# Windowed attention followed by a gated channel mix: some transposes moved to the DMA crossbar, casts moved between engines, deeper pools, a split last product, and another order

## The chip, the cores and the metric

The kernel runs on one core of one Trainium2 chip. The metric is the time of one execution on the device in microseconds (us), median of several runs; lower is better. The profile is one more execution under the hardware profiler, and its span runs from the first to the last instruction, so it is about 1.7 us shorter than the time of the same run. Engines are PE (TensorE, with PEld for its weight loads), DVE (VectorE), ACT (ScalarE), POOL (GpSimd) and SP (the engine whose queue issues most DMAs). A run counts as slow when it is over 1.5% above the fastest of its kernel, else as fast; ratios use fast runs alone.

## The reference

```python
# q, k, v: (4, 8, 768, 64) f32; window 128, 4 sink positions; weights w_k 512x1024, w_v 1024x512, w_r 512x512
scores = where(keep, q @ k.T / 8, -1e9)       # keep: first 4 positions, or 0 <= row - col < 128
a = softmax(scores);  x = heads side by side of (a @ v)          # (4, 768, 512)
x_prev = x shifted down by one row in each batch
xk = mu_k*x + (1-mu_k)*x_prev;  xr = mu_r*x + (1-mu_r)*x_prev
out = sigmoid(xr @ w_r) * (relu(xk @ w_k)**2 @ w_v)
```

## The kernel before

The work is cut into 12 units of 256 rows (4 batches of 3). A unit goes through: load q, k, v; cast to bf16; transpose q and k; scores, exponential, mask, values; normalise to x; transpose x; shift and mix into xk and xr; then keys (`kp`), gate (`rp`) and product (`vp`) with the weights. Every operation is registered in a plan with its engine, the buffers it takes and a number. `ORDER` lists for each engine the numbers in the order in which it issues them, and that order was found by a search beforehand. Each engine's program is written in this order, so an operation that waits holds up everything that is listed behind it.

```python
CAST = {"k": "ACT", "q": "DVE"}      # who casts k and q of units 1 to 11
KD = range(4, 12)                    # units whose k is transposed by the DMA crossbar
QD = ()                              # ... and whose q: none
ORDER = {"PE": (88, 85, 101, ...), "DVE": (...), "ACT": (...), "POOL": (...), "SP": (...)}
# ... cut
pool("sc", TOGETHER, [128, 2, 512], FP32, psum)        # TOGETHER = 2
pool("bank", 8 - 2 * TOGETHER, [128, 512], FP32, psum)
pool("kb", 2, ...); pool("qb", 2, ...); pool("kt", 3, ...); pool("qt", 2, ...); pool("e", 4, ...)
pool("es", 2, ...); pool("rec", 3, ...); pool("x", 2, ...); pool("xk", 2, ...); pool("xr", 2, ...)
pool("rl", 3, ...)
# ... cut: prepare(u), for each half of q and of k
copy(out=buf[rk][:, half], in_=buf[raw][:, hs])        # the cast, on DVE or ACT
if by_dma(name, u):                                    # the crossbar: SP issues, no engine computes
    nc.sync.dma_start_transpose(out=buf[key][:, :, half, :], in_=buf[rk][:, half])
    continue
nc.tensor.transpose(out=ps[:, i, j, :], in_=..., identity=ident)   # four of them on PE, then
nc.scalar.copy(out=buf[key][...], in_=buf[psk][...])               # the evacuation on ACT
# ... cut: ffn(u), for each half g of the rows
for f in range(4 * part, 4 * part + 4):                # product: 8 matmuls of 512 columns
    nc.tensor.matmul(out=buf[psk], rhs=wv_h[:, f, :], lhsT=buf["kk", u][:, f, 128*g:128*g+128], ...)
nc.vector.scalar_tensor_tensor(out=buf[bk], in0=buf[tk], scalar=1.0, in1=buf[psk],
                               op0=ALU.add, op1=ALU.mult)
nc.sync.dma_start(out=out[b, s0:s0 + 128, :], in_=buf[bk])
# ... cut: where the plan sees PE idle in the first 45 us and a PSUM bank free, it puts a filler
P.fill = lambda bank: nc.tensor.matmul(out=bank, lhsT=warm[:, 0:128], rhs=warm, start=True, stop=True)
```

The softmax here doesn't subtract the row's maximum and nothing guards it: scores larger than these inputs give would overflow.

## Time and profile before

| | before |
|---|---|
| time, median | 178.24 us of 3 runs; 177.93 us of 4 beside the changed kernel |
| span of the profile | 177.0 us (that run took 178.66 us) |
| busy: PE, DVE, ACT | 164.5, 154.3, 127.4 us |
| mean granted clock of PE | 0.977 |
| packets on the DMA engines, share of 16 engines' span | 75% on the main queue |

How to read it: PE's busy share is high, but it adds up matmuls that overlap: a key product lasts 276 ns on the mean, and in full stretches the next one starts 109 ns later.

### The profile page before, as it was taken

How to read it: one execution, taken by the hardware profiler on the slowest of the kernel's cores; microseconds unless marked ns; L12 is line 12 of the kernel's file. 1: busy time of each engine (PE TensorE's matmuls, PEld its weight loads, DVE VectorE, ACT ScalarE, POOL GpSimd, SP SyncE). 2: the span in 40 equal slices, each digit the busy share in tenths (PEclk: the TensorE clock that was granted, in tenths of full speed). 3: DMA queues.
4: the chain of work that ended last, by engine and by line, in shares of the span. 5: the costliest groups of instructions: out<-in, count | busy, mean ns of one | idle time of the engine just before them, and what ended most of it. 6: DMA issues, size and time to landing. Idle time of an engine off the chain costs nothing.

```text
span 177.0 us, 4245 instructions
## 1 busy us (share of the span) xinstructions
PE 164.5 (93%) x1619; PEld 109.8 (62%) x1640; DVE 154.3 (87%) x393; ACT 127.4 (72%) x205; POOL 25.1 (14%) x47
## 2 busy tenths in 40 slices
PE   7996579899998999999999999999999999999991
PEld 2444357685656758757657659557668577664840
DVE  6377997999999989999999998999899999778522
ACT  2168895989496995999876887888998764844240
POOL 6004100009131010114110031401120000000000
PEclk9999957999999999999999999999999999999998
DMA  5999999979957988979994799799862010040403
GB/s 150 261 226 250 346 383 386 332 180 258 232 129 191 283 117 205 235 147 265 211 264 126 201 274 249 139 240 137 225 156 70 4 59 0 4 178 0 178 4 119
DMA packets 74148, 32.79 MB, mean 185 GB/s; under 512 B 52112, under 2 KB 68496, under 8 KB 74128
## 3 DMA queue, kind: packets, MB, share of 16 engines
q1 hardware_dynamic: 73072, 32.51, 75.0%
q8 instruction: 13, 0.21, 0.5%
q10 hardware_dynamic: 1056, 0.00, 0.3%
q14 instruction: 7, 0.06, 0.1%
HBM read 24.12 MB, written 6.29 MB: 172 GB/s over the span
## 4 chain that ended last, share of the span: by engine, by line
PE 71%; DVE 17%; DMA 3%; SPq 3%; issue 2%; ACT 1%; ACTq 0%; DVEq 0%
PE bank L778 21%; PE bank L816 21%; PE bank L801 10%; PE bank L695 6%; PE sc L636 5%; DMA qs<-in_q_dram 3%; DVE xk L757 3%; DVE e L672 3%; PE bank L551 3%; PE bank L734 2%; DVE xr L757 2%; PE bank L683 2%; SPq L378 2%; DVE kk L791 2%; PE bank L612 2%
## 5 line engine op out<-in xcount | busy, mean ns | idle before, releaser
L778 PE MATMUL bank<-xk,wk_sb 128*128 128x256 bf16 x384 | 51.5, 276 | 1.9 <-DVE wk_sb L504 1.3
L658 ACT ACTIVATE e<-sc 128x1024 bf16<-128x1024 f32 (+1 forms) x48 | 45.4, 966 | 3.8 <-PE sc L636 3.7
L816 PE MATMUL bank<-wv_h,kk 128*128 128x512 bf16 x181 | 46.6, 379 | 0.5
L778 PEld LDWEIGHTS <-wk_sb 128*128 128x128 bf16 x384 | 35.8, 99 | 10.4 <-issue 1.7
L787 ACT ACTIVATE rl<-bank 128x512 bf16<-128x512 f32 x48 | 27.9, 603 | 15.8 <-PE bank L778 14.5
L576 POOL CAST vb<-vs 128x512 bf16<-128x512 f32 x22 | 17.9, 822 | 103.5 <-DMA vs<-in_v_dram 90.2
L672 DVE TENSOR_TENSOR e<-e,mask 128x1024 bf16<-128x1024 bf16 (+1 forms) x48 | 31.1, 652 | 0.5 <-ACT e L658 0.5
L816 PEld LDWEIGHTS <-kk 128*128 128x128 bf16 x192 | 17.4, 98 | 15.1
L801 PE MATMUL bank<-wr_sb,xr 128*128 128x512 bf16 x87 | 23.9, 379 | 1.0 <-ACT xt L742 0.4
L791 DVE TENSOR_TENSOR kk<-rl 128x512 bf16<-128x512 bf16 x48 | 20.8, 448 | 3.5 <-ACT rl L787 3.0
L757 DVE SCALAR_TENSOR_TENSOR xr<-td,mu,xt 128x256 bf16<-128x256 bf16 x48 | 23.5, 499 | 0.0
L757 DVE SCALAR_TENSOR_TENSOR xk<-td,mu,xt 128x256 bf16<-128x256 bf16 x48 | 22.4, 486 | 0.1
L695 PE MATMUL bank<-vb,e 128*128 128x65 bf16 x352 | 20.3, 197 | 0.8 <-ACT kt L561 0.6
L711 DVE TENSOR_TENSOR x<-bank,rec 128x256 bf16<-128x256 f32 x48 | 19.8, 418 | 0.6
L807 ACT ACTIVATE th<-bank 128x512 f32<-128x512 f32 x24 | 14.4, 612 | 8.2 <-PE bank L801 8.2
L695 PEld LDWEIGHTS <-e 128*128 128x128 bf16 x352 | 17.6, 100 | 3.3 <-DVE e L672 1.1
L825 DVE SCALAR_TENSOR_TENSOR ob<-th,bank 128x512 f32<-128x512 f32 x24 | 16.3, 680 | 3.8 <-PE bank L816 3.7
L742 ACT COPY xt<-bank 128x512 bf16<-128x512 bf16 x24 | 14.1, 590 | 5.5 <-PE bank L734 5.5
L561 ACT COPY qt<-bank 128x512 bf16<-128x512 bf16 x22 | 16.4, 748 | 1.6 <-PE bank L551 1.3
L801 PEld LDWEIGHTS <-xr 128*128 128x128 bf16 x96 | 9.0, 98 | 8.7 <-DVE xr L757 0.6
L636 PE MATMUL sc<-qt,kt 64*128 64x128 bf16 (+1 forms) x256 | 14.3, 243 | 0.0
L683 PE MATMUL bank<-vsink,es 128*128 128x130 bf16 x64 | 13.3, 229 | 0.0
(49 smaller groups left out, 153.0 us busy)
## 6 DMA issues: line engine op xcount, KB each, us to landing
vs<-in_v_dram SPq DMA_DIRECT2D x24, 256.0 KB, 5.3
out_dram<-ob SPq DMA_DIRECT2D x24, 256.0 KB, 2.5
qs<-in_q_dram SPq DMA_DIRECT2D x11, 512.0 KB, 6.0
ks<-in_k_dram SPq DMA_DIRECT2D x18, 256.0 KB, 4.7
wk<-in_moe_w_k_dram SPq DMA_DIRECT2D x2, 1024.0 KB, 10.4
wv<-in_moe_w_v_dram SPq DMA_DIRECT2D x2, 1024.0 KB, 12.9
ks<-in_k_dram SPq DMA_DIRECT2D x3, 512.0 KB, 9.1
wr<-in_moe_w_r_dram SPq DMA_DIRECT2D x1, 1024.0 KB, 10.6
```

What stands on the lines that cost most here:

```text
L576: lambda g=g, copy=copy: copy(out=buf["vb", u][:, g, :, 0:D], in_=buf["v", u][:, g, :, :]), rank,
L636: nc.tensor.matmul(out=sc[:, a, o0:o1], lhsT=lhs[rows], rhs=rhs[rows], start=True, stop=True)
L658: nc.scalar.activation(out=buf[ek][:, :, lo:], in_=buf[sck][:, :, lo:], func=AF.Exp, scale=scale)
L672: nc.vector.tensor_tensor(out=at, in0=at, in1=m, op=ALU.mult)
L695: nc.tensor.matmul(out=o[:, g, a, :], lhsT=e[:, a, e0:e0 + 128], rhs=rhs, start=(T == 0 and i == 0), stop=(i == len(blocks) - 1), skip_gro ...
L711: P.op("DVE", dve(256), lambda ok=ok, rk=rk, c=c: nc.vector.tensor_tensor(out=buf["x", u][:, :, 128 * c:128 * c + 128].rearrange("p g (a d ...
L757: nc.vector.scalar_tensor_tensor(out=buf[key][:, c0 + i, :], in0=buf[tk][:, i, :], scalar=mu[w][:, c0 + i:c0 + i + 1], in1=xt[:, c0 + i, t ...
L778: nc.tensor.matmul(out=ps[:, i, :], lhsT=wk_sb[:, c, 128 * f:128 * f + 128], rhs=xk[:, c, :], start=(c == 0), stop=(c == NC - 1), skip_gro ...
L787: P.op("ACT", act(512), lambda psk=psk, rk=rk: nc.scalar.activation(out=buf[rk], in_=buf[psk].rearrange("p (i t) -> p i t", i=2), func=AF. ...
L791: P.op("DVE", dve(512, 0.52), lambda f2=f2, rk=rk: nc.vector.tensor_tensor(out=buf["kk", u][:, 2 * f2:2 * f2 + 2, :], in0=buf[rk], in1=buf ...
L801: nc.tensor.matmul(out=buf[psk], lhsT=buf["xr", u][:, c, 128 * g:128 * g + 128], rhs=wr_sb[:, c, :], start=(c == 0), stop=(c == NC - 1))
L816: nc.tensor.matmul(out=buf[psk], rhs=wv_h[:, f, :], lhsT=buf["kk", u][:, f, 128 * g:128 * g + 128], start=(f == 0), stop=(f == NF - 1))
```

## The change

Its intent: take work off PE where PE is the bound (q of units 8 to 11 through the DMA crossbar), take casts off DVE and give them to ACT, give the order more buffers, shorten the tail, and find the order again for all this.

```diff
-CAST = {"k": "ACT", "q": "DVE"}
+CAST = {"k": "ACT", "q": "ACT"}
-QD = ()
+QD = range(8, 12)
 ORDER = {   # every engine's line is another one (cut)
-    pool("kb", 2, ...)  pool("qb", 2, ...)  pool("kt", 3, ...)  pool("qt", 2, ...)  pool("e", 4, ...)
+    pool("kb", 3, ...)  pool("qb", 3, ...)  pool("kt", 4, ...)  pool("qt", 3, ...)  pool("e", 5, ...)
-    pool("es", 2, ...)  pool("rec", 3, ...)  pool("x", 2, ...)  pool("xk", 2, ...)  pool("xr", 2, ...)
+    pool("es", 3, ...)  pool("rec", 6, ...)  pool("x", 3, ...)  pool("xk", 3, ...)  pool("xr", 3, ...)
-    pool("rl", 3, ...)
+    pool("rl", 4, ...)
+    def last_product(rank):            # unit 11, second half of the rows
+        for part in range(2):          # 256 columns each: 8 matmuls, one DVE step, one store
+            cols = slice(256 * part, 256 * part + 256)
+            ... nc.tensor.matmul(out=buf[psk][:, 0:256], rhs=wv_h[:, f, cols], ...)
+            ... scalar_tensor_tensor(out=buf[bk][:, 0:256], in0=buf[tk][:, cols], ...)
+            ... dma_start(out=out[B - 1, S - 128:S, cols], in_=buf[bk][:, 0:256])
+            if (u, g) == (U - 1, 1):
+                last_product(rank); continue
# cut: a branch for x through the crossbar, which no unit uses (XD = ())
```

## The prediction

> **What bounds the kernel now.** I read the page's busy table first, then the stage table (busy time of each engine per 10 us), the clock of TensorE in 1 us steps, the groups by shape, and last the chain that ended last, in order of time. From the page:
>
> ```profile
> PE 164.5 (93%) x1619; PEld 109.8 (62%) x1640; DVE 154.3 (87%) x393; ACT 127.4 (72%) x205; POOL 25.1 (14%) x47
> ...
> PEclk9999957999999999999999999999999999999998
> DMA  5999999979957988979994799799862010040403
> ```
>
> TensorE is the busiest, VectorE second, and at one point of the ramp the granted clock drops. The stage table says where TensorE is short of full:
>
> ```profile
> 10.00:20.00 10.00, 6.97 (x83) 4.03 (x82) 8.41 (x24) 7.96 (x12) 2.91 (x7) 1.00 1.09 273
> 20.00:30.00 10.00, 8.25 (x97) 6.51 (x98) 8.87 (x23) 7.19 (x12) 0.00 (x0) 0.66 1.06 373
> 30.00:40.00 10.00, 9.20 (x86) 7.07 (x86) 10.00 (x24) 8.98 (x16) 0.24 (x1) 1.00 0.95 269
> ...
> 100.00:110.00 10.00, 9.95 (x105) 6.97 (x105) 9.35 (x24) 8.04 (x13) 1.43 (x2) 1.00 1.06 234
> ```
>
> Columns after the stretch: PE, PEld, DVE, ACT and POOL busy, then clock, DMA share, GB/s. From about 44 us on PE is full; before that it is not, while DVE is near full and the DMA share is 1. Two long stretches, with the same columns:
>
> ```profile
> 5.90:44.00 38.10, 32.42 (x317) 21.78 (x319) 32.57 (x78) 29.65 (x47) 7.16 (x10) 0.91 1.03 292
> 44.00:173.30 129.30, 127.48 (x1292) 86.29 (x1307) 117.81 (x302) 96.51 (x158) 14.57 (x24) 1.00 0.70 155
> ```
>
> In the second, PE is idle 1.8 us of 129.3. So the time is: ramp (first transpose at 5.9 us, full at 44), PE's own work, and a tail of 3.7 us (last product ends 173.3, span 177.0).
>
> Useful PE work, from start-to-start times in PE's timeline where it is full (busy sums count pipelined matmuls too long): keys 384 x 0.109 = 41.9; last product 192 x 0.216 = 41.5; gate 96 x 0.216 = 20.7; attention values 32 x 0.36 + 16 x 0.18 = 14.4; scores 16 x 0.55 + 8 x 0.44 = 12.3; input transposes 32 groups of four x 0.225 = 7.2; transposes of x 24 x 0.225 = 5.4; sink scores 8 x 0.44 = 3.5; sink values 0.9. Sum 147.8 us. Between 5.9 and 173.3 us there are 167.4 us, so 19.6 us are not useful: 1.8 after 44 us, and about 17.8 in the ramp. Of those, 5.7 are idle (38.1 - 32.4), some 5 are filler matmuls (about 23 of the 36 lie after 5.9 us, at 0.216), and much of the rest is the half clock:
>
> ```profile
> 22.00:23.00 1.00, 0.99 (x13) 0.65 (x12) 1.00 (x3) 0.87 (x3) 0.00 (x0) 0.52 1.05 376
> ...
> 27.00:28.00 1.00, 1.00 (x9) 0.82 (x8) 0.69 (x2) 0.00 (x0) 0.00 (x0) 0.50 1.06 391
> 28.00:29.00 1.00, 1.00 (x20) 1.00 (x18) 0.18 (x2) 0.73 (x1) 0.00 (x0) 0.57 1.02 375
> ```
>
> It runs at 0.50 from about 22.0 to 28.85 us, 6.83 us, after PE had stood idle from 18.5 to 20.0. This is worth up to 3.4 us. The first key product starts only at 25.81 us, released by DVE's cast of the weights; in the chain of waits that stretch is one DVE instruction after another:
>
> ```profile
> 23.69 0.25 DVE wk_sb L504
> 23.94 0.28 issue
> 24.22 0.38 DVE xr L757
> 24.60 0.02 issue
> 24.62 0.16 DVE rec L708
> 24.78 0.37 DVE xk L757
> 25.15 0.61 DVE wk_sb L504
> ```
>
> **What the Trainium skill says.** (1) "TensorE: Matmul & The Clock Gate", Part 1: the clock is halved after an idle activity window of 3413 ns. The trace agrees in size: the dip is 6.83 us, two such windows. (2) "ScalarE: Activation LUTs", What ACT_TABLE_LOAD costs: 186 ns + 0.833 ns per element and row; for 512 that is 612 ns, and the casts of k took 632 ns. So a cast of q on ACT costs the same. (3) "DMA: Bandwidth & Descriptors", Specifications: pieces below 512 B don't reach line rate. The trace's packets agree: 256 B took 21.2 ns on the mean and 512 B took 30.3, so half the bytes at 0.70 of the time. Its HBM limit of about 358 GB/s was exceeded here (391 in the row above); I use the measurement.
>
> **The change, part by part.**
>
> ```profile
> L551 PE MATMUL bank<-ident,qb 128*128 128x128 bf16 x96 | 9.1, 219 | 1.8 <-DVE qb L530 1.5 <-DVE vsink L599 0.3
> L561 ACT COPY qt<-bank 128x512 bf16<-128x512 bf16 x22 | 16.4, 748 | 1.6 <-PE bank L551 1.3
> L530 DVE CAST qb<-qs 128x512 bf16<-128x512 f32 x24 | 9.8, 418 | 3.2 <-DMA qs<-in_q_dram 3.2
> ```
>
> 1. *q of units 8 to 11 by the crossbar.* PE loses 8 groups of 4 transposes: 8 x 0.225 = **1.8 us**, all in the stretch where PE is the bound, so it counts in full. ACT loses 8 evacuations x 748 = 6.0 us. The DMA engines get 8 crossbar transposes (512 packets of 256 B: 512 x 21.2 / 16 = 0.68 us each, 5.4) and four loads in 256 B pieces (2048 x 21.2 / 16 = 2.71 for 1024 x 30.3 / 16 = 1.94 us, 3.1 in all): 8.5 us more on a queue whose share over 44 to 173 us is 0.70. The input loads end near 131 us in the page's DMA row, so there is room after them. The issuing queue gets 8 x 1.2 us more.
>
> 2. *Casts of q from DVE to ACT.* 22 of 24 casts: DVE loses 22 x 0.418 = 9.2 us of busy time (7.5 at its start-to-start pace of 0.34), ACT gains 22 x 0.632 = 13.9. With part 1, DVE goes from 154 to 145, ACT from 127 to 127.4 + 13.9 - 6.0 = 135. Off the path once PE is full; in the ramp, where DVE is dense, four casts leave before 25 us and one more by 44, 5 x 0.34 = 1.7 us.
>
> 3. *Order and deeper pools.* The order of instructions shows: all of unit 0's q and k is asked for before anything of unit 1; both halves of the key weights stand before v of unit 1, so 2 MB after 2.5 MB of other data rather than the second half after 6. On DVE three of the four casts of key weights now come before unit 1's masks, and 24 key matmuls stand on PE before unit 1's attention values, where before 8 came amid them. Fillers go from 36 to 44; the last eight stand just where PE idled before the dip. From the last x of unit 0 (17.8 us before; I take 15 to 16.5, as loads for unit 0 come first) DVE needs about 3.5 us for two xr and xk pairs and casts (6 x 0.39 + 2 x 0.6) until the key products can start: near 20 us for 25.8. Not all of that is won: DMA moves at 373 GB/s already, so the total brought in by 31 us can't rise, and eight more fillers take 1.7 us. My sum for the ramp: fillers 6.7, idle 2 to 3, clock 0 to 2, cold start and switching 4: about 14.2 for 17.8, **3.6 us won**. This is the softest term.
>
> 4. *Last product in column halves.* The last DVE step shrinks from 0.69 us to about 0.42 (the 256-wide row of x), 0.3 won, and the last store is half as large: about **0.5 us** in all. Its 16 matmuls of 256 columns cost what 8 of 512 do (0.109 against 0.216 / 2).
>
> 5. *New friction.* ACT at 78% and crossbar data needed late: I charge 1 us.
>
> Sum: 1.8 + 3.6 + 0.5 - 1.0 = 4.9 off 178.24 is 173.3. As the clock dip has its own chance to vanish whole, I put the centre at **172.8 us**.
>
> **The rivals.** (a) *The ramp is set by the loads.* DMA share about 1 and 373 GB/s speak for it; then only bytes matter and earlier key weights merely delay v, gate and product weights. Gain 1.8 + 0.5 + about 1: 175. Against it: at 23 to 25 us the chain runs through DVE, not DMA. (b) *ACT becomes the bound.* Its busy time was 9.79 in the stretch 70 to 80 us and 9.47 in the next; two more casts per unit (1.3 us in units 1 to 7, where no evacuation is saved) overfill it locally. PE would wait for evacuations: 2 to 4 us lost, 175 to 177. Against it: deeper pools let such work move, and ACT still ends at 78%. (c) *Crossbar late.* Unit 11's q comes after 8.5 us more DMA; if issue stalls behind a store, scores of units 9 to 11 wait. Against it: at the end PE holds about 14 us of other work. (d) *Everything goes well:* key products at 20 us and PE full from there: with about 6 us of useful work done by then, 146 - 6 + 20 + 1.8 + 3.4 ends near 165 in the trace, 167 timed. DVE (145 us of work) would hardly let it.
>
> **Range and chances.** (a) and (b) end at 175 to 177, the sum at 173, half of (d) at 169. Range **169.5 to 176.5**. The line of 2% is 174.7. Chances: faster by over 2% **0.70**, within 2% **0.27**, slower **0.03**, for nothing is added to PE and only a stall could lose time.
>
> **What would show it.** Part 1: 64 and not 96 q transposes on PE, busy some 2 us less. Part 2: DVE near 145 and ACT near 135 us. Part 3: the first key product near 20 us, no or a shorter dip of the clock, PE full from about 40 us. Part 4: a tail near 3.2 us. Part 5: PE idle after 44 us not above 3 us. I am wrong if PE waits in mid-kernel for ACT's evacuations or a crossbar landing, if the dip only moves, or if the ramp gains far more than 3.6 us.

## The result and the profile after

The changed kernel took **171.84 us** (171.66 to 172.17, 4 runs) beside 177.93 us (177.46 to 178.62, 4 runs). The ratio is **0.9657**, with a 95% interval of 0.9617 to 0.9697. A ratio is the mean time of one kernel's fast runs over that of the other's of the same rounds, so it is not quite the ratio of the medians. On two other occasions (different chips are used) the ratio of the same kernel was 0.9703 and 0.9705, so the gain is 5.3 to 6.1 us. The prediction was 172.8 us with a range of 169.5 to 176.5.

The page of the changed kernel, busy times and slices, to be put beside the first fence of the prediction:

```profile
PE 161.4 (95%) x1603; PEld 107.9 (63%) x1624; DVE 149.4 (88%) x372; ACT 132.5 (78%) x219; POOL 25.1 (15%) x47
...
PEclk9999999999999999999999999999999999999999
DMA  4999999999959899999858998999989974030203
```

DVE lost 4.9 us and ACT gained 5.1 (the prediction had DVE near 145 and ACT near 135 us). The dip of the clock is gone, and the loads run on for some slices longer. The two long stretches of the changed kernel, ramp and full stretch (PE, PEld, DVE, ACT, POOL busy, clock, DMA share, GB/s):

```profile
44.00:166.73 122.73, 121.81 (x1223) 83.58 (x1235) 112.24 (x280) 98.01 (x165) 14.77 (x22) 1.00 0.84 172
5.38:44.00 38.62, 35.52 (x375) 22.70 (x378) 35.23 (x87) 33.21 (x54) 6.64 (x12) 1.00 1.07 297
```

PE's last matmul now ends at 166.73 us and not at 173.3. Useful work is now 147.8 - 1.8 = 146.0 us, and from the first transpose to the last matmul there are 161.35 us, so 15.35 us are not useful; 0.92 of them after 44 us, 14.4 before. PE's timeline in the ramp of the changed kernel (start, length, what, how many):

```profile
18.27 0.63 PE L611 MATMUL bank<-qt,ksink 128*128 128x256 bf16 x4
18.95 1.72 PE L879 MATMUL bank<-warm 128*128 128x512 bf16 x7
20.61 0.76 PE L635 MATMUL sc<-qt,kt 64*128 64x256 bf16 x12
21.30 2.79 PE L818 MATMUL bank<-xk,wk_sb 128*128 128x256 bf16 x24
```

The first key product starts at 21.30 us (25.81 before), and 24 stand there at a stretch. The fillers (`warm`) fill the place at which PE had idled. The groups of q by shape:

```profile
L529 ACT CAST qb<-qs 128x512 bf16<-128x512 f32 x14 | 8.6, 639 | 0.0
L550 PE MATMUL bank<-ident,qb 128*128 128x128 bf16 x64 | 6.0, 219 | 1.0 <-DVE x L710 0.3 <-ACT xt L744 0.3 <-ACT kt L560 0.3
L526 ACT CAST qb<-qs 128x512 bf16<-128x512 f32 x8 | 5.0, 622 | 1.1 <-DMA qs<-in_q_dram 1.1
```

64 transposes of q are left on PE where 96 were, and 22 casts are on ACT. The end of the chain, first of the kernel before:

```profile
171.49 1.74 PE bank L816 x8
173.31 0.69 DVE ob L825
```

and of the changed one:

```profile
164.97 1.76 PE bank L788 x16
166.75 0.42 DVE ob L798
```

The last DVE step went from 0.69 to 0.42 us, and from the last matmul to the end of the span there are 3.2 us instead of 3.7.

So the 7.1 us between the two spans are made up of: PE work removed 1.8, non-useful time in the ramp 17.8 - 14.4 = 3.4, idle time after 44 us 1.8 - 0.9 = 0.9, a first transpose that starts 0.5 us earlier (5.38 for 5.9), and 0.5 in the tail. The profiled run of before was a long one of its kind (178.66 us), and the medians differ by only 5.3 to 6.1 us. In which of these terms the remaining 1.0 to 1.8 us lie is not known, so no term is sure to better than that.

### The profile page after: what moved, and what is told of

It is laid out like the page before. It is cut to its first block, busy times and chain, and to the rows that moved or that the text cites.

```text
span 169.9 us, 4214 instructions
## 1 busy us (share of the span) xinstructions
PE 161.4 (95%) x1603; PEld 107.9 (63%) x1624; DVE 149.4 (88%) x372; ACT 132.5 (78%) x219; POOL 25.1 (15%) x47
## 3 DMA queue, kind: packets, MB, share of 16 engines
q1 hardware_dynamic: 81728, 33.56, 86.8%
## 4 chain that ended last, share of the span: by engine, by line
PE 81%; DVE 6%; DMA 5%; SPq 4%; issue 1%; ACT 1%; DVEq 0%
PE bank L818 24%; PE bank L859 23%; PE bank L841 12%; PE sc L635 6%; PE bank L694 6%; DMA wk<-in_moe_w_k_dram 5%; PE bank L733 3%; SPq L377 3%; PE bank L550 2%; PE bank L682 2%; PE bank L611 2%; SPq L360 1%; DVE e L671 1%; DVE wk_sb L503 1%; PE bank L788 1%
## 5 line engine op out<-in xcount | busy, mean ns | idle before, releaser
L818 PE MATMUL bank<-xk,wk_sb 128*128 128x256 bf16 x384 | 48.9, 273 | 0.0
L859 PE MATMUL bank<-wv_h,kk 128*128 128x512 bf16 x173 | 45.3, 379 | 0.6
L575 POOL CAST vb<-vs 128x512 bf16<-128x512 f32 x22 | 18.4, 845 | 111.4 <-DMA vs<-in_v_dram 101.4
L671 DVE TENSOR_TENSOR e<-e,mask 128x1024 bf16<-128x1024 bf16 (+1 forms) x48 | 31.6, 669 | 0.4 <-ACT e L657 0.4
L859 PEld LDWEIGHTS <-kk 128*128 128x128 bf16 x184 | 16.6, 98 | 14.7 <-DVE kk L831 0.3
L694 PE MATMUL bank<-vb,e 128*128 128x65 bf16 x352 | 18.9, 193 | 0.4 <-DVE e L671 0.4
L694 PEld LDWEIGHTS <-e 128*128 128x128 bf16 x352 | 16.7, 97 | 2.8 <-DVE e L671 0.6
L868 DVE SCALAR_TENSOR_TENSOR ob<-th,bank 128x512 f32<-128x512 f32 x23 | 15.7, 682 | 2.1 <-ACT th L847 1.7
L879 PE MATMUL bank<-warm 128*128 128x512 bf16 x42 | 12.3, 423 | 1.4 <-DVE warm L894 1.3
L635 PEld LDWEIGHTS <-kt 64*128 64x128 bf16 x256 | 8.9, 94 | 6.1 <-issue 3.7
```

Of the source, the lines that this page charges most:

```text
L575: lambda g=g, copy=copy: copy(out=buf["vb", u][:, g, :, 0:D], in_=buf["v", u][:, g, :, :]), rank,
L635: nc.tensor.matmul(out=sc[:, a, o0:o1], lhsT=lhs[rows], rhs=rhs[rows], start=True, stop=True)
L671: nc.vector.tensor_tensor(out=at, in0=at, in1=m, op=ALU.mult)
L694: nc.tensor.matmul(out=o[:, g, a, :], lhsT=e[:, a, e0:e0 + 128], rhs=rhs, start=(T == 0 and i == 0), stop=(i == len(blocks) - 1), skip_gro ...
L818: nc.tensor.matmul(out=ps[:, i, :], lhsT=wk_sb[:, c, 128 * f:128 * f + 128], rhs=xk[:, c, :], start=(c == 0), stop=(c == NC - 1), skip_gro ...
```

## The experiments

Twelve runs were made, two of them controls, all with correct results. A difference "over the control" is (ratio / ratio of the control - 1) x 172.4 us. The first four ran together on one chip, the next four on another with a control of its own. The last four ran on the chip of the first four, but at another time, and are read against that control (0.9703). Where work was put in as a dummy, the order of all other operations stayed as it was. Such a kernel is no kernel that anyone would write, but it shows what one amount of work costs at one place.

The mean clock of a run says whether the dip happened in it. In the traces, 0.988 to 0.99 goes with one stretch of 3.4 us at half clock (runs 3, 7, 8), 0.977 to 0.981 with two (the kernel before, run 12), and 0.998 or more with none before the last matmul; 0.995 leaves no room for one, as half of 3.4 us is 0.01 of a run. The profile of the kernel before shows two; of its 27 runs beside run 1, 16 had about 0.99 and 11 had 0.981 or less.

**1. The control.** The changed kernel as it is.

> The changed kernel as it is, as a control on the same chip as the three runs beside it: 0.966 of the time of before (0.962 to 0.970), about 171.8 us. Every theory expects the same here; the other runs of this call are read against it.

Measured: 172.35 us beside 177.76; ratio 0.9703 (0.968 to 0.9727).

**2. The last product whole again.**

```diff
-            if (u, g) == (U - 1, 1):
-                last_product(rank)
-                continue
```

> The changed kernel with its last product whole again (8 matmuls of 512 columns, one VectorE step, one store), everything else and the order kept. Theory: the column halves are worth the 0.5 us by which the tail after the last matmul shrank (3.7 to 3.2 us), so this run is 0.4 to 0.6 us longer than the control (172.2 to 172.4 us). Rival: the tail is set by the fixed latency of the last store and the difference lies in noise, under 0.2 us.

Measured: 173.01 us, ratio 0.974 (0.9716 to 0.9764), which is 0.7 us over the control. In its chain the last DVE step is 0.69 us again. The halves are worth what their tail shows, 0.5 to 0.7 us.

**3. Fillers off in the ramp of the changed kernel.**

```diff
-    P.fill_until = 45000.0
+    P.fill_until = 15500.0     # the last eight of 44 fillers are not issued
```

> The changed kernel without its last eight filler matmuls (those at 18.9 to 20.6 us); PE then stands idle about 1.7 us there. Theory: without them the granted clock falls to a half for some 3.4 to 6.8 us from about 22 us, and since PE has a queue of key products there, the time rises by 1 to 3 us. Rival: the ramp is set by loads and VectorE; the clock may fall, but the time stays within 0.5 us of the control. If the clock doesn't fall at all, the fillers do nothing and the time is the same.

Measured: 173.55 us, ratio 0.9773, 1.2 us over the control; mean clock 0.988. The same place of its timeline:

```profile
20.70 0.40 PE L636 MATMUL sc<-qt,kt 64*128 64x256 bf16 x6 [1.18 <-ACT kt L561]
21.58 0.61 PE L636 MATMUL sc<-qt,kt 64*128 64x256 bf16 x6 [0.49 <-ACT e L658]
22.12 4.15 PE L819 MATMUL bank<-xk,wk_sb 128*128 128x256 bf16 x24
```

The brackets hold the idle time before an instruction and who ended it. PE stood idle 1.18 and 0.49 us, the clock fell, and the same 24 key products took 4.15 us rather than 2.79: 1.36 us more. PE has its work ready at that moment, so the half clock is paid there. The profiled run is the longest of the six (174.23 us). One of the six kept its clock (0.998) and took 172.84 us; the other five took 173.75 on the mean. So about 0.9 us goes with the dip, by that one run. Without the fillers the key products start no earlier either: 22.12 us, in the control 21.92.

**4. The kernel before, with fillers against the dip.** Thirteen matmuls of 256 columns into columns that nobody reads, where PE had been idle from 18.5 to 20.0 us.

```diff
+    for i in range(13):
+        P.op("PE", 112.0, lambda i=i: nc.tensor.matmul(out=buf["xtp", 0, 1][:, 256:512],
+             lhsT=warm[:, 0:128], rhs=warm[:, 0:256], start=True, stop=True, ...), ...)
     # ORDER: these thirteen behind the second transposition of x of unit 0
```

> The kernel before with thirteen filler matmuls of 256 columns (0.109 us each, 1.4 us) where PE stands idle from 18.5 to 20.0 us, nothing else changed. Theory: the half clock from 22.0 to 28.85 us goes and that alone gives 1 to 2.5 us of the 6.1 us, as VectorE waited 1.1 us on PE in it. Rival: VectorE paces the ramp there, so the time stays within 0.5 us of before.

Measured: 177.85 us (22 runs) beside 177.76 (27 runs), ratio **1.0004** (0.9985 to 1.0022). On the mean the time is the same, so the theory failed as a forecast. In the profiled run the dip is gone (mean clock 0.999). The stage table in the ramp of the kernel before:

```profile
24.00:28.00 4.00, 2.72 (x22) 2.07 (x20) 3.69 (x10) 2.71 (x5) 0.00 (x0) 0.50 1.05 389
28.00:32.00 4.00, 3.25 (x51) 2.68 (x49) 3.18 (x9) 3.01 (x5) 0.00 (x0) 0.89 1.04 382
```

and of this run:

```profile
24.00:28.00 4.00, 2.15 (x37) 1.79 (x34) 4.00 (x12) 3.50 (x6) 0.00 (x0) 1.00 1.04 387
28.00:32.00 4.00, 3.44 (x45) 2.37 (x42) 4.00 (x11) 3.42 (x5) 0.00 (x0) 1.00 1.06 385
```

At the full clock (the third number from the end: 0.50 became 1.00) PE is busy less of the same 4 us (2.15 for 2.72) and DVE all of it. The first key product starts no earlier, before and in this run:

```profile
25.81 1.89 PE L778 MATMUL bank<-xk,wk_sb 128*128 128x256 bf16 x8 [1.28 <-DVE wk_sb L504]
25.89 1.05 PE L779 MATMUL bank<-xk,wk_sb 128*128 128x256 bf16 x8 [1.60 <-DVE wk_sb L505]
```

PE got faster and waited longer for DVE's cast of the weights: at this place the half clock was hidden behind DVE. But 3 us later DVE in its turn had waited for the slow PE, and that wait is gone in this run. The first line is of the kernel before; the second is this run's, more than 100 us later:

```profile
28.82 0.18 DVE L708 RECIPROCAL rec<-bank 128x4 f32<-128x4 f32 x1 [1.13 <-PE bank L695]
PE bank L696 <- ACT xt L743: 1.2, 1, 1.2
```

From there on this run is 1.0 to 1.5 us ahead of the profile of before (DVE's `ob` step, the last of a half unit, starts at 42.81 for 43.95 us the first time and at 114.55 for 115.58 the thirteenth). At 131.5 us it loses that and more: PE waits 1.2 us for a copy of x on ACT that stands behind a chain of DVE's work. So the dip was not hidden in the ramp; what it cost there was lost again at the second bound. This profile is also one of the two longest of the 22 runs (179.1 us).

The run is not as clean as it looks. Seven of the 22 runs still had a dip (clock 0.988 to 0.99): they took 178.39 us on the mean, the 15 without it 177.58. So 0.8 us goes with one stretch of half clock in this kernel too. And 178.39 is 0.7 us more than the kernel before took with one stretch (177.65, 16 runs): the thirteen matmuls seem to cost something themselves (PE's next transpositions start at 20.51 for 20.03 us), and the two cancel. Comparing runs by their clock is not an experiment, but it speaks against the reading that the half clock costs nothing in the old order and counts only in the new one.

**5. A second control**, for the next three.

> The changed kernel as it is, control of this call: 0.966 to 0.970 of the time of before. The three runs beside it are read against it.

Measured: 172.37 us, ratio 0.9705 (0.9674 to 0.9737).

**6. PE's work put back.** Eight groups of four dummy matmuls behind the transpositions of x of units 8 to 11.

```diff
+    for u in range(8, 12):
+        for half in range(2):      # four matmuls of 128 columns, into columns that nobody reads
+            P.op("PE", 225.0, dummy, 0, ...)
```

> The changed kernel with eight groups of four dummy matmuls of 128 columns on PE (0.225 us a group, 1.8 us in all), one behind each transposition of x of units 8 to 11, into columns that nothing reads. They weigh what the q transposes weighed that the crossbar took over. Theory: PE is the bound there, so the whole 1.8 us comes back (1.5 to 2.1 us over the control). Rival: PE's stretch waits for other engines in hidden ways and part of it is absorbed: under 1.0 us.

Measured: 174.2 us, ratio 0.9819 (0.9781 to 0.9857), 2.0 us over the control (1.8 by the medians). All of the 1.8 us come back: PE's work in the full stretch counts one to one, within some 0.9 us by the two intervals. ACT's evacuations and the DMA were not put back with it.

**7. DVE's casts put back.** 22 dummy casts on DVE, from and into storage of weights that are already cast.

```diff
+    for u in range(1, U):
+        for half in range(2):
+            P.op("DVE", ..., lambda: nc.vector.tensor_copy(
+                out=wk32[:, 0, 0:256].bitcast(BF16), in_=wk32[:, 1, 0:512]), ...)
     # ORDER: each where the cast of q of its unit stands on ACT
```

> The changed kernel with 22 dummy casts of 128x512 on VectorE (0.34 us each at its pace, 7.5 us in all) where the real casts of q now run on ScalarE (the first three as soon as the key weights are cast, about 25 us), on data that nobody reads afterwards. Theory: VectorE at 88% busy is a near second bound; with 95% it holds up PE in the ramp and in its full stretches, +2 to +5 us over the control. Rival: VectorE ran ahead all along and the relief was worth nothing: within 0.5 us of the control.

Measured: 177.36 us (22 runs, one of them slow and left out of the ratio), ratio 0.9996 (0.9973 to 1.0019): **5.2 us** over the control for 7.5 us of work. This is as much as nearly the whole gain of the change. A part of it is that the dip came back in the profiled run and others: eight runs without it (clock 0.997 and more) took 176.81 us on the mean, twelve with one stretch 177.72. So 4.5 us over the control come without the dip. The run adds work to DVE and takes none from ACT, so it does not say what moving the casts was worth; with ACT as full as run 8 shows, that can be much less, and no run moved them back.

**8. ACT's casts of units 1 to 7 doubled.** As run 7, with `nc.scalar.copy`, 14 of them.

> The changed kernel with 14 dummy casts of 128x512 on ScalarE (0.63 us each, 0.55 at its pace, about 7.7 us) where the casts of q of units 1 to 7 stand, so that stretch carries each of them twice. It tries my rival that ScalarE becomes the bound: it was busy 9.6 to 10.0 of 10 us between 30 and 80 us. Theory: it is at its limit there but PE has other work queued, so +0.5 to +3 us. Rival (ScalarE is the second bound): +4 to +8 us, all of it. If nothing comes (under 0.3 us), ScalarE's busy share says little.

Measured: 179.04 us, ratio 1.0086 (1.0056 to 1.0116): **6.8 us** over the control for about 7.7 us of work. The rival's forecast holds. The stage table of the control, 40 to 80 us:

```profile
40.00:60.00 20.00, 19.84 (x210) 13.10 (x212) 18.64 (x49) 19.20 (x36) 3.39 (x6) 1.00 0.97 219
60.00:80.00 20.00, 19.89 (x209) 14.37 (x210) 17.92 (x39) 19.89 (x33) 4.76 (x5) 1.00 1.26 228
```

and of this run:

```profile
40.00:60.00 20.00, 18.96 (x190) 12.40 (x192) 18.03 (x45) 19.60 (x36) 2.82 (x6) 1.00 0.74 162
60.00:80.00 20.00, 19.15 (x180) 12.35 (x180) 14.58 (x36) 20.00 (x38) 2.72 (x4) 1.00 1.13 230
```

In the control PE and ACT are both full. With more on ACT, PE loses 1.6 us in these 40 us and DVE is starved. 78% over the span hid an engine that has little to spare for 50 us. But a good part of the 6.8 us arose before: the third copy of x starts at 32.05 us for 29.18 in the control. There the first dummies waited 0.88 us for DVE's last cast of the key weights, and three stood in a row; and the clock dipped once in five of the six runs (0.99). Run 10 has neither.

**9. Only the late DVE casts put back** (units 4 to 11, 16 casts, 5.4 us, after about 48 us): run 7 with `range(4, U)`.

> The changed kernel with the dummy VectorE casts of units 4 to 11 alone (16 casts, 5.4 us, all after about 48 us); the six in the ramp are left out. It splits the 5.0 us that all 22 cost. Theory of my prediction: once PE is full VectorE's casts lie beside it, so under 0.5 us over the control (0.970 of before), and the 5.0 us came from the six casts in the ramp. Rival: VectorE is a second bound throughout, so its share by count comes back, 2.5 to 4 us over the control.

Measured: 175.29 us, ratio 0.9846 (0.9807 to 0.9885): 2.5 us over the control, so about half of the work shows. It lies at the edge of what the rival expected and far from the theory. The other 2.7 us of run 7 belong by difference to six casts in the ramp (2.0 us of work; the clock's dip is in that too). The chain that ended last between 44 and 150 us, its shares by line, for the changed kernel:

```profile
by line: PE bank L859 29.3%; PE bank L818 28.8%; PE bank L841 13.7%; PE sc L635 8.3%; PE bank L694 7.4%; PE bank L733 3.9%; PE bank L611 2.7%; PE bank L682 2.7%; PE bank L550 2.0%; issue 0.8%; PE bank L594 0.6%
```

and for run 9 (lines shifted by one; cut at its end):

```profile
by line: PE bank L860 21.3%; PE bank L819 19.1%; PE bank L842 9.6%; PE sc L636 6.3%; PE bank L695 4.7%; DVE e L672 4.2%; DVE ob L869 4.0%; DVE xk L769 3.8%; PE bank L734 3.1%; DVE xr L769 3.1%; DVE x L711 3.0%; DVE wk L896 2.6%; PE bank L61
```

In the changed kernel the chain is PE's alone. With the casts on DVE, masks, stores' last steps, mixes and the dummies (`wk`) come into it: DVE is next in line behind PE over the whole kernel, not in the ramp alone. In the trace the delay against run 1 grows with the dummies: 0.65 us at 59 us, 2.0 at 108, 3.0 at 144.

**10. Only the ACT casts of units 4 to 7 doubled** (8 casts, 4.4 us at 48 to 70 us): run 8 with `range(4, 8)`.

> The changed kernel with the dummy ScalarE casts of units 4 to 7 alone (8 casts, 4.4 us at their pace, at about 48 to 70 us), where ScalarE's busy share is 9.6 to 10 of 10 us. All 14 cost 6.7 us. Theory: PE holds other work there, under 1 us over the control, and the ramp took the rest. Rival: ScalarE is as much the bound as PE there: 3 to 4.5 us.

Measured: 175.35 us, ratio 0.9861 (0.9828 to 0.9895), 2.8 us over the control: 0.6 of the work shows. This is just under the rival's range and far from the theory; ACT, too, is next behind PE there. In the trace the whole delay arises where the dummies stand: 2.7 us against run 1 at 84 us, and no more after that.

**11. Pools back to their old sizes**, all but the transposed q.

```diff
-    pool("kb", 3) ("qb", 3) ("kt", 4) ("e", 5) ("es", 3) ("rec", 6) ("x", 3) ("xk", 3) ("xr", 3) ("rl", 4)
+    pool("kb", 2) ("qb", 2) ("kt", 3) ("e", 4) ("es", 2) ("rec", 3) ("x", 2) ("xk", 2) ("xr", 2) ("rl", 3)
```

> The changed kernel with all its deeper pools back to the sizes of before, but for the transposed q (3, as with 2 the order has no way to go on); order and all else kept. Theory: the order was found with these pools and takes them up, so waits for buffers come back: 0.5 to 3 us over the control (0.970 of before). Rival: the pools only make room that the order rarely uses: within 0.4 us.

Measured: 173.25 us, ratio 0.975 (0.9712 to 0.9788), 0.8 us over the control; the two intervals overlap, so the sign is likelier than the size. With the old pool of transposed q this order can't run at all: the kernel's own planner stops with "no operation can go on", as some engine waits for a buffer whose release stands behind it. So this order needs that pool; what an order found for the old pools would reach is open, and the new order was never tried by itself.

**12. A version meant to beat both.** Gate and product weights cast by DMAs that GpSimd issues, so DVE has six casts fewer in the ramp.

```diff
-    P.op("SP", ..., lambda: nc.sync.dma_start(out=wv32[...], in_=src), ...)    # then a cast on DVE
+    P.op("POOL", ..., lambda: nc.gpsimd.dma_start(out=wv_h[...], in_=src), ...)   # f32 to bf16 on the way
-    func=AF.Relu)
+    func=AF.Relu, scale=0.5 ** 0.5)        # the half that had been in the cast
     # ORDER: repaired for it by a short search
```

> A version meant to beat the changed kernel: the gate and product weights are cast to bf16 by DMAs that GpSimd issues (the half that was folded into the cast goes into the scale of the rectifier, the square root of a half), so VectorE loses six casts of 0.60 us in the ramp, where casts put back cost time; the order was repaired for it. If VectorE sets the ramp, 1 to 3 us under the control (0.970 of before); if the loads or ScalarE set it, within 0.7 us; if casting DMAs are slow and weights come late, 1 to 3 us over it.

Measured: 179.59 us, ratio 1.01, 7.1 us over the control: far worse, beyond the worst that I had set down. The table of DMA issues (KB each, median us to landing) of the changed kernel:

```profile
ks<-in_k_dram SPq DMA_DIRECT2D x3, 512.0 KB, 8.1
```

and of this run:

```profile
ks<-in_k_dram SPq DMA_DIRECT2D x3, 512.0 KB, 18.9
wr_sb<-in_moe_w_r_dram POOLq DMA_DIRECT2D x1, 512.0 KB, 11.3
```

On one queue the weights had stood in the place that the order gave them. On a second queue they ran beside the loads of k, and those took 18.9 us to land for 8.1; PE then stood 4.07 us at a stretch, released by ACT's cast of that k:

```profile
35.29 0.61 PE L548 MATMUL bank<-ident,kb 128*128 128x128 bf16 x4 [4.07 <-ACT kb L527]
```

The clock dipped in all six runs as well (0.967 to 0.986). The search had also moved other operations, so how much of the 7 us is the queue's alone is open. The changed kernel stays the fastest.

## Why the prediction was right or wrong

**Right in the total, with some luck in the parts.** The time of 171.84 us is 1.0 us from 172.8 and inside the range. The prediction forecast 5.4 us (4.9, and 0.5 for the dip); the times say 5.3 to 6.1, the two profiled spans 7.1. One term had the wrong sign, and one reason was wrong.

1. *Transposes to the crossbar, 1.8 us.* Right, and for PE's work shown by putting it back (run 6: 2.0 us).
2. *The ramp, 3.6 us.* The size was right by the two profiles: non-useful time fell from 17.8 to 14.4 us, so 3.4. Its terms came near too: idle 3.1 us (38.62 - 35.52; 2 to 3 expected), clock 0 (0 to 2), fillers about 31 x 0.216 = 6.7 (6.7), the rest 4.6 (4). PE is full from about 32 us on, not 40. The key products start at 21.3 us and not near 20. The eight fillers ahead of them (seven in this trace's records) are not the reason, for without them they start no earlier (run 3); there the scores ahead of them waited for ACT (1.18 and 0.49 us). One reason was wrong: "This is worth up to 3.4 us", said of the dip, and the half microsecond by which I moved the centre for it. Taking the dip out of the kernel before won nothing on the mean (run 4), and between runs of one kernel one stretch of half clock goes with 0.3 to 0.9 us, where half its length is 1.7. What came with the gain is that DVE lets PE go earlier: its first two casts of the key weights start at 17.5 and 18.8 us and not at 23.6 and 25.1. No run takes this order back alone, so its worth is known by difference only. The last eight fillers of the changed kernel are worth 1.2 us (run 3).
3. *The tail, 0.5 us.* Right (0.5 in the trace, 0.7 in run 2).
4. *New friction, minus 1 us.* Wrong in sign. The failed step is "Off the path once PE is full", said of DVE's casts. PE's idle time after 44 us fell from 1.8 to 0.9 us, and putting the late casts back costs 2.5 us (run 9). In the changed kernel DVE is a second bound over the whole length; at 1.8 us of PE idle in 129.3 that could not be seen before, because PE's share shows who is first and not how close the next one is. That DVE had been so close in the kernel before is likely by run 4, where PE waits behind DVE at 131.5 us, but not shown. By the sum of the spans, plus 0.9 came where I had put minus 1.0, and a start 0.5 us earlier was left out. Against that stands the half microsecond that I had added for the dip. What moving the casts contributed to the plus 0.9 is open: runs 7 and 9 add to DVE, runs 8 and 10 add to ACT, and none moves them back.
5. *Rival (b), ACT as the bound.* It did not happen, as PE's 9.9 of 10 us and the control show, but the reason I gave against it ("ACT still ends at 78%") was worthless: 7.7 us more on ACT cost 6.8 us (run 8, the ramp and a dip included), 4.4 us cost 2.8 (run 10). There was little more that ACT could have taken in units 4 to 7.
6. *Rival (a), the loads.* The load order was not tried by itself, so its part in the ramp is open. That arrival order matters in this ramp is made likely by run 12, in which late k cost PE 4 us.
7. *DMA's 8.5 us more.* Mis-sized: the queue's packets took 86.8% of 169.9 = 147.5 us of 16 engines where they had taken 75.0% of 177.0 = 132.8, so 14.7 more. By the packet records 256 B pieces account for 17.9 more and 512 B pieces for 7.2 less, so 10.7 where I had 8.5; 3.0 us more went to 4-byte packets, which I had not counted. No cost is seen: PE's idle time did not grow.
8. *Part 2's busy times.* DVE came to 149.4 us and not 145, ACT to 132.5 and not 135. The casts moved as counted (the q casts on DVE fell from 9.8 to 0.9 us, and the two groups on ACT take 13.6); why the sums moved less was not looked into. The prediction's 612 ns for a cast on ACT is an estimate; the casts of q took 639 and 622 ns there.

## What to carry to other kernels

A kernel in which one engine is full can have two more that are full just behind it: put dummy work on an engine and see how much of it comes back before moving work there, or taking credit for moving it away. A slow clock or a slow instruction is worth at most the time that it adds; look at who releases the instruction after it, and again at where the next wait eats what was won. If a state such as the dip comes and goes between runs, compare the runs that have it with those that don't. And an order is found for one set of buffers and one queue of loads: both belong to it, and changing one alone can cost more than the change was to win.

## What the Trainium skill lacked or had wrong

- "TensorE: Matmul & The Clock Gate", Terms, puts the penalty at about the throttled time multiplied by (1 - K/N). For one stretch of 3.4 us at half clock that is an estimate of 1.7 us. Between runs of one kernel, 0.9 us went with one stretch in run 3 (one run against five), 0.8 in run 4 and 0.9 in run 7; in the kernel before, a second stretch went with 0.3 to 0.4. Here the product is an upper bound, since PE waited for others anyway for a part of it.
- The same page, HAM oscillation, warns of PE idle gaps above about 3.4 us. Here the clock fell after shorter ones: 1.5 us idle at 18.5 to 20.0 us in the kernel before, and gaps of 1.18 and 0.49 us in run 3; in the 3.4 us before the fall PE was busy for 1.55 and 1.80 us. How busy a window must be to count as busy, the page does not say, beyond its remark in Part 4 that transposes don't count in the same way.
- "DMA: Bandwidth & Descriptors", Specifications, has about 358 GB/s as the HBM limit of a core without a condition; further down, in Measured, the page ties it to both cores of a pair streaming and has more for a lone core. The kernel before moved 391 GB/s in a stretch of 1 us and 389 over 4 us, which fits the second statement.
- The same page's part on the DMA transpose (X-bar) has no time for one such transpose on trn2 from SBUF to SBUF. In the kernel before a half of k, 128 by 512, took SP's queue 1.21 us to issue and 3.1 us in the median from issue to landing.
- The same page, SWDGE vs HWDGE vs iDMA, names GpSimd as the only issuer of a DMA that casts, and says that DMAs of all issuers interleave on the same engines, but has no figure for what such loads do to others: in run 12 loads of k on the other queue took 18.9 us in the median to land, where 8.1 had been usual.
- No page that I read says how to tell a second bound hidden behind a full engine; busy shares did not (DVE 88%, ACT 78%), and dummy work did: 2.5 us of 5.4, and 2.8 us of 4.4, came back (runs 9 and 10).
